# Twenty of the thirty-two rows of `wo` on each partition loaded by two GpSimd transfers of 120 partitions

## The chip, the cores and the metric

The kernel runs on one core of one Trainium2 chip. Its time is device microseconds of that core for one execution; the time before is the median of three runs. A profile is one execution of the program recorded by the hardware; its span runs from the first to the last instruction, and the execution's own time is a little longer.

The core has four engines that compute (TensorE, VectorE, ScalarE and GpSimd, in the profile PE, DVE, ACT and POOL), SyncE (SP), which here issues nearly all loads, and sixteen DMA engines that move the bytes. A transfer that SP issues is queue q1 in the profile, one that GpSimd issues is queue q0.

## The reference

One token passes an attention block over a long cache and a gated feed-forward block, side by side. All arrays are float32.

```python
x = A_x                                   # 1 x 1 x 576
xn = layernorm(x)
q = (xn @ wq).reshape(1, 1, 32, 128)      # 32 heads of 128
p = softmax(q . k_cache * 128**-0.5)      # 16384 keys a head
o = p . v_cache                           # 32 x 128
h = gelu(xn @ w_gate) * (xn @ w_up)       # 4608
out = x + o.reshape(4096) @ wo + h @ w_down
```

The two caches hold 268 MB each (32 x 16384 x 128 floats), `wo` (4096 x 576) and the three weights of the feed-forward block some 9 to 11 MB each. Every byte is used once.

## The kernel before

**Order of the work.** Lines 67 to 120 load `wq` and work out the query of all heads. Then a loop over 64 tiles of keys (two a head, 128 partitions of 64 keys) loads a tile of `k_cache` (line 178) and, three tiles later, the tile of `v_cache` that belongs to it (line 182). VectorE and ScalarE make the scores (lines 191 to 196), TensorE multiplies the probabilities with the values (line 226). The weights of the gate and of the up projection are loaded between tiles, in the first 12 of them.

**The end.** After the last tile comes the part that the change touches. Each step multiplies one column of 128 activations with 128 rows of a weight and adds into the accumulator `acc` in PSUM (`add_out`, line 297). `w_down` comes first, in three loads of 12 rows of 576 floats a partition (3456 KB each). Then the 32 x 128 attention output `oall` is transposed (line 315), copied to `orow` (line 317) and turned by a GpSimd transfer into `oT`, 128 partitions by 32 columns (line 319). Two GpSimd transfers bring `x` into `x2` (line 324). `wo` is laid out with 32 rows of 576 floats on each partition, and loaded in four pieces of 12, 12, 6 and 2 rows a partition. The piece of two rows is itself cut over the partitions into six transfers, of 8, 4, 2, 1, 112 and 1 partitions (`LAST`). Each row of a partition takes two calls of the matmul, for the two halves of 288 outputs, and each call shows as two matmuls in the profile: 48 for 12 rows, 40 for 10. Once 30 rows are in, VectorE copies half of the accumulator out (line 337) and TensorE adds it back to the other half (line 339); the last two rows follow, then `x` is added (line 342) and the result stored (line 343).

**What sets the order.** All large loads go into a ring of five buffers of 32 KB a partition, named `slot`. A load is issued when its buffer's last reader is done: the first two pieces of `wo` take the buffers of the last but one and the last tile of values, the third piece that of the first piece of `w_down`, the fourth that of the second. SP and GpSimd each issue in order; the DMA engines take what is queued, each at its own pace, and a load counts as landed when all engines that carry a share of it are done. TensorE works the pieces off in the order of the program. Where a transfer waits for nothing, the scheduler may issue it far earlier than the program has it.

Of the kernel before, what the change touches and what calls it, by code (L numbers as in the profile page):

```python
# [8 lines left out]
F32 = mybir.dt.float32  # L9
# [4 lines left out]
P = 128  # L14
H, SK, DH = 32, 16384, 128
D, DF = 576, 4608
# [12 lines left out]
HALF = D // 2  # L29
# [2 lines left out]
FQ = FS // 4  # L32
FT = FS // P
WO_T = H * DH // P
LAST = (8, 4, 2, 1, 112, 1)


@with_exitstack
def kernel(ctx: ExitStack, tc: tile.TileContext, x, k_cache, v_cache, wq, wo, wg, wu, wd, out):
    nc = tc.nc  # L40
    cpool = ctx.enter_context(tc.tile_pool(name="cpool", bufs=1))
# [9 lines left out]
    xf = x.rearrange("b s d -> (b s) d")  # L51
# [3 lines left out]
    wov = wo.rearrange("(p t) f -> p t f", t=WO_T)  # L55
    wdv = wd.rearrange("(s p t) f -> s p t f", p=P, t=FT)

    def slot():
        return slots.tile([P, R * DH], F32, tag="s", name="slot")
# [93 lines left out]
    hT = cpool.tile([P, DF // P], F32, name="hT")  # L153
# [140 lines left out]
    def add_out(j, lhs, w, last=False):  # L294
        for i in range(2):
            q = 32 * (2 * (j % 2) + i)
            nc.tensor.matmul(acc[q : q + 1, :HALF], lhs,  # L297
                             w[:, i * HALF : (i + 1) * HALF], start=q not in seen, stop=last)
            seen.add(q)

    def load_rows(src, n, cuts=(P,)):
        w = slot()[:, : n * D]
        p = 0
        for c in cuts:
            nc.sync.dma_start(w[p : p + c, :], src[p : p + c, :])
            p += c
        return w.rearrange("p (t f) -> p t f", f=D)

    for s in range(DF // FS):
        w = load_rows(wdv[s].rearrange("p t f -> p (t f)"), FT)  # L310
        for j in range(FT):
            add_out(j, hT[:, s * FT + j : s * FT + j + 1], w[:, j, :])

    po = ps_s.tile([P, 512], F32, tag="sm", name="pot")
    nc.tensor.transpose(po[:H, :P], oall, ident)
    orow = cpool.tile([H, P], F32, name="orow")
    nc.scalar.activation(orow, po[:H, :P], AF.Copy)
    oT = cpool.tile([P, WO_T], F32, name="oT")
    nc.gpsimd.dma_start(oT, orow)

    x2 = cpool.tile([P, HALF], F32, name="x2")
    nc.vector.memset(x2, 0.0)
    for i in range(2):
        nc.gpsimd.dma_start(x2[32 * i : 32 * i + 1, :], xf[:, i * HALF : (i + 1) * HALF])

    lo = 0
    for n in (12, 12, 6, 2):
        end = lo + n == WO_T
        w = load_rows(wov[:, lo : lo + n, :].rearrange("p t f -> p (t f)"), n, LAST if end else (P,))
        for j in range(n):  # L330
            add_out(0 if end else j, oT[:, lo + j : lo + j + 1], w[:, j, :],
                    last=lo + j in (WO_T - 3, WO_T - 1))
        lo += n
        if lo == WO_T - 2:
            part = cpool.tile([P, HALF], F32, name="part")
            nc.vector.memset(part, 0.0)
            nc.vector.tensor_copy(part[64:], acc[64:, :HALF])  # L337
            for i in range(2):
                nc.tensor.matmul(acc[32 * i : 32 * i + 1, :HALF], ident[:, 64 + 32 * i : 65 + 32 * i], part,
                                 start=False, stop=False)  # L340
# [31 lines left out]
```

## Time and profile before

| | |
|---|---|
| median of three runs | 1396.02 us (1395.83 to 1396.08) |
| the profiled execution | 1396.48 us |
| its span | 1394.7 us |
| bytes moved from HBM in the span | 587.60 MB |
| VectorE busy | 956.3 us |
| TensorE busy | 527.9 us |
| ScalarE busy | 536.1 us |
| GpSimd busy | 14.2 us |
| largest rate in a fortieth of the span | 438 GB/s |

The page of the profile gives first the busy time of each engine and then the span in 40 slices, with the busy share of the DMA engines in tenths and the bytes that they moved. A view by windows gives, for any stretch of the span, the busy time of an engine, the mean share of the sixteen DMA engines that was busy, and GB/s: one busy engine of sixteen is a share of 0.06. The chain of waits follows the last instruction back to what released it.

### The profile page before, as it was taken

The page shows a single profiled execution, that of the slowest core. Times are in us where ns is not written, and L with a number is a line of the kernel's source. Part 1 is how long each engine was busy: PE and PEld are TensorE (multiplying, and loading weights), DVE is VectorE, ACT ScalarE, POOL GpSimd, SP SyncE. Part 2 cuts the span into 40 slices and gives each one's busy share as a digit, 9 for nine tenths or more (in the row PEclk, how much of TensorE's full clock was granted, in tenths as well). Part 3 has the DMA queues.
Part 4 walks back from the last instruction along what each step waited for, and adds up shares of the span by engine and source line. Part 5 has one row for each costly group of instructions (what it writes and reads, how often), then busy time and mean ns, then how long its engine had stood idle before and what let it go on. Part 6 is the DMA issues. An engine that isn't in the chain of part 4 may idle for free.

```text
span 1394.7 us, 10849 instructions
## 1 busy us (share of the span) xinstructions
PE 527.9 (38%) x3071; PEld 151.4 (11%) x3071; DVE 956.3 (69%) x634; ACT 536.1 (38%) x3251; POOL 14.2 (1%) x33
## 2 busy tenths in 40 slices
PE   6634234344234323342243323332333233332575
PEld 3211001011001000000011000100011001100121
DVE  1977565739877877778777877787777777787500
ACT  0644333325443444344344434444434433443300
POOL 0000000000000000000000000000000000000000
PEclk9866667565665665656656566665666666656677
DMA  9999999999999999999999999999999999999993
GB/s 406 422 426 431 422 432 428 419 438 429 428 432 435 425 432 434 429 430 435 431 428 433 430 432 430 432 430 431 432 432 430 430 433 430 431 432 430 430 428 124
DMA packets 25618, 588.36 MB, mean 422 GB/s; under 512 B 3267, under 2 KB 3285, under 8 KB 7254
## 3 DMA queue, kind: packets, MB, share of 16 engines
q1 hardware_dynamic: 24692, 587.61, 98.4%
q8 instruction: 24, 0.39, 0.1%
q14 instruction: 36, 0.29, 0.1%
q0 software_dynamic: 864, 0.06, 0.0%
q10 hardware_dynamic: 2, 0.00, 0.0%
HBM read 587.60 MB, written 0.00 MB: 421 GB/s over the span
## 4 chain that ended last, share of the span: by engine, by line
DMA 72%; DVE 20%; PE 7%; issue 1%; POOL 0%; SPq 0%; ACT 0%; DVEq 0%
DMA slot<-in_A_k_cache_dram 34%; DMA slot<-in_A_v_cache_dram 34%; DVE slot L191 12%; DVE s L196 7%; PE po L226 5%; DMA slot<-in_A_wo_dram 3%; DMA gu<-gc 2%; PE pg L144 1%; PE acc L297 1%; POOL gu L151 0%; PE pt L206 0%; DVE pm L202 0%; PE pb L212 0%; PE pl L233 0%; SPq L63 0%
## 5 line engine op out<-in xcount | busy, mean ns | idle before, releaser
L191 DVE TENSOR_TENSOR slot<-slot,q 128x2048 f32<-128x2048 f32 x256 | 574.5, 2286 | 259.4 <-DMA slot<-in_A_k_cache_dram 259.3
L226 PE MATMUL po<-slot,pe 128*4 128x512 f32 x2048 | 372.0, 893 | 758.1 <-DMA slot<-in_A_v_cache_dram 758.1
L195 ACT ACTIVATE jk<-slot 128x128 f32<-128x128 f32 x1536 | 453.2, 296 | 521.7 <-DVE slot L191 518.5
L196 DVE TENSOR_REDUCE s<-slot 128x10 f32<-128x1280 f32 x256 | 367.7, 1478 | 0.0
L195 ACT ACTIVATION_READ_ACCUMULATOR jk<-slot 128x1 f32 x1536 | 286.8, 187 | 0.0
L226 PEld LDWEIGHTS po<-slot,pe 128*4 128x4 f32 x2048 | 60.2, 111 | 1015.7 <-DMA slot<-in_A_v_cache_dram 749.6
L245 PE MATMUL pc<-sel,o 128*128 128x1 f32 x256 | 35.3, 259 | 39.6 <-ACT o L239 39.6
L239 ACT ACTIVATE o<-po 128x512 f32<-128x512 f32 x32 | 19.0, 595 | 78.5 <-PE po L226 78.5
L214 ACT ACTIVATE nb<-pb 128x1 f32<-128x1 f32 x32 | 5.5, 171 | 95.6 <-PE pb L212 95.6
L337 DVE COPY part<-acc 64x288 f32<-64x288 f32 x1 | 0.5, 461 | 60.7 <-PE acc L297 60.7
L245 PEld LDWEIGHTS pc<-sel,o 128*128 128x128 f32 x256 | 32.6, 199 | 71.2 <-ACT o L239 71.2
L117 PE MATMUL pq<-slot,xnb 128*128 128x512 f32 x64 | 31.6, 641 | 7.9 <-DMA slot<-in_A_wq_dram 7.9
L235 DVE RECIPROCAL rl<-pl 128x1 f32<-128x1 f32 x32 | 5.4, 169 | 38.2 <-PE pl L233 38.2
L210 DVE TENSOR_REDUCE nm<-pt 1x1 f32<-1x128 f32 x32 | 8.9, 278 | 30.3 <-PE pt L206 30.3
L249 ACT ACTIVATE oall<-pc,rl 128x1 f32<-128x1 f32 x32 | 8.4, 261 | 38.2 <-PE pc L245 38.2
L144 PE MATMUL pg<-slot,xnb 128*32 128x384 f32 x192 | 21.0, 588 | 0.9 <-DMA slot<-in_B_w_up_dram 0.6
L120 ACT ACTIVATE q<-pq 128x512 f32<-128x512 f32 x8 | 4.8, 597 | 38.9 <-PE pq L118 38.9
L212 PE MATMUL pb<-nm,ones 1*128 1x1 f32 x64 | 12.0, 255 | 14.6 <-DVE nm L210 14.6
L297 PE MATMUL acc<-slot,oT 128*1 128x288 f32 x128 | 12.9, 559 | 9.8 <-DMA slot<-in_A_wo_dram 9.8
L206 PE MATMUL pt<-ident,pm 128*1 128x128 f32 x32 | 8.9, 280 | 20.0 <-DVE pm L202 19.8
L117 PEld LDWEIGHTS pq<-slot,xnb 128*128 128x128 f32 x64 | 13.2, 208 | 24.5 <-issue 24.5
L297 PE MATMUL acc<-slot,hT 128*1 128x288 f32 x144 | 12.5, 510 | 6.4 <-DMA slot<-in_B_w_down_dram 6.4
(60 smaller groups left out, 131.3 us busy)
## 6 DMA issues: line engine op xcount, KB each, us to landing
slot<-in_A_k_cache_dram SPq DMA_DIRECT2D x64, 4096.0 KB, 43.0
slot<-in_A_v_cache_dram SPq DMA_DIRECT2D x64, 4096.0 KB, 34.6
slot<-in_B_w_down_dram SPq DMA_DIRECT2D x3, 3456.0 KB, 38.0
slot<-in_B_w_gate_dram SPq DMA_DIRECT2D x3, 3072.0 KB, 43.9
slot<-in_B_w_up_dram SPq DMA_DIRECT2D x3, 3072.0 KB
slot<-in_A_wq_dram SPq DMA_DIRECT2D x2, 4096.0 KB, 14.4
slot<-in_A_wo_dram SPq DMA_DIRECT2D x2, 3456.0 KB
slot<-in_A_wo_dram SPq DMA_DIRECT2D x1, 1728.0 KB, 33.4
```

What stands on the lines that cost most here:

```text
L117: nc.tensor.matmul(pq, xnb[:, j, :], wv[:, j, g * 512 : (g + 1) * 512], start=j == 0, stop=False)
L144: nc.tensor.matmul(pg[32 * q : 32 * q + 32, :FQ], lhs, rhs, start=j == 0, stop=j == DJ)
L191: nc.vector.tensor_mul(blk, blk, Q[h].to_broadcast([P, SUB, DH]))
L195: nc.scalar.activation(jk, blk[:, n, :], AF.Copy, accum_out=S[h][:, o + n : o + n + 1])
L196: nc.vector.tensor_reduce(S[h][:, o : o + nv], blk[:, :nv, :], axis=AX.X, op=ALU.add)
L206: nc.tensor.transpose(PT[h][:1, :P], PM.pop(h), ident)
L210: nc.vector.tensor_reduce(nm, PT.pop(h)[:1, :P], axis=AX.X, op=ALU.max, negate=True)
L212: nc.tensor.matmul(pb[:, :1], ones[:1, :], nm, start=True, stop=True)
L226: nc.tensor.matmul(OP[h][q : q + 4, :], PE_[h][:, k : k + 4], vt[:, n * DH : (n + 4) * DH], start=k < 16, stop=k >= C * R - 16)
L239: nc.scalar.activation(OS[h], OP.pop(h), AF.Copy)
L245: nc.tensor.matmul(PC[h][:, :1], o4[:, j * DH : (j + 1) * DH], sel[:, j : j + 1], start=j == 0, stop=j == 3)
L297: nc.tensor.matmul(acc[q : q + 1, :HALF], lhs, w[:, i * HALF : (i + 1) * HALF], start=q not in seen, stop=last)
```

## The change

The first 20 of the 32 rows of each partition come in two loads of ten rows. Of each, GpSimd loads partitions 0 to 119 and SP the remaining eight. A row of ten is taken as two halves of five rows (11,520 bytes), kept apart in the buffer by a gap of 32 floats. Ahead of the first, between the two and behind the second stands a tiny GpSimd transfer (`turn`), which reads 2, 17 and 15 pieces of `x` into a scratch tile `pad`. The other 12 rows come by SP in loads of ten and two, now of all 128 partitions each. `pool_dma` ties each GpSimd transfer behind the GpSimd instruction that stands before it in the program; the transfers of `oT` and of `x2` are now issued through it as well.

```diff
-LAST = (8, 4, 2, 1, 112, 1)
+PART = 120
+GAP = 32
...
-    def load_rows(src, n, cuts=(P,)):
+    def load_rows(src, n):
         w = slot()[:, : n * D]
-        p = 0
-        for c in cuts:
-            nc.sync.dma_start(w[p : p + c, :], src[p : p + c, :])
-            p += c
-        return w.rearrange("p (t f) -> p t f", f=D)
+        nc.sync.dma_start(w, src)
+        w = w.rearrange("p (t f) -> p t f", f=D)
+        return [w[:, j, :] for j in range(n)]
+
+    pad = cpool.tile([P, 48], F32, name="pad")
+
+    def pool_dma(dst, src):
+        tc.keep_in_program_order(nc.gpsimd.dma_start(dst, src))
+
+    def turn(k):
+        pool_dma(pad[:k].rearrange("p (a f) -> p a f", f=16)[:, 0:3:2, :],
+                 xf[:, : k * 32].rearrange("o (k a f) -> (o k) a f", a=2, f=16))
+
+    def load_part(src, n):
+        half = n // 2 * D
+        w = slot()[:, : 2 * (half + GAP)].rearrange("p (a f) -> p a f", a=2)[:, :, :half]
+        src = src.rearrange("p (a f) -> p a f", a=2)
+        pool_dma(w[:PART], src[:PART])
+        nc.sync.dma_start(w[PART:], src[PART:])
+        return [w[:, j // (n // 2), j % (n // 2) * D : (j % (n // 2) + 1) * D] for j in range(n)]
...
-    nc.gpsimd.dma_start(oT, orow)
+    pool_dma(oT, orow)
...
-        nc.gpsimd.dma_start(x2[32 * i : 32 * i + 1, :], xf[:, i * HALF : (i + 1) * HALF])
+        pool_dma(x2[32 * i : 32 * i + 1, :], xf[:, i * HALF : (i + 1) * HALF])

     lo = 0
-    for n in (12, 12, 6, 2):
+    for n in (10, 10, 10, 2):
         end = lo + n == WO_T
-        w = load_rows(wov[:, lo : lo + n, :].rearrange("p t f -> p (t f)"), n, LAST if end else (P,))
+        src = wov[:, lo : lo + n, :].rearrange("p t f -> p (t f)")
+        if lo < 20:
+            turn(17 if lo else 2)
+            w = load_part(src, n)
+        else:
+            w = load_rows(src, n)
...
         lo += n
+        if lo == 20:
+            turn(15)
```

More of the change, by code (lines that the diff above doesn't have):

```diff
@@ L311 @@
         for j in range(FT):
-            add_out(j, hT[:, s * FT + j : s * FT + j + 1], w[:, j, :])
+            add_out(j, hT[:, s * FT + j : s * FT + j + 1], w[j])
     po = ps_s.tile([P, 512], F32, tag="sm", name="pot")
@@ L323 @@
     for i in range(2):
-        nc.gpsimd.dma_start(x2[32 * i : 32 * i + 1, :], xf[:, i * HALF : (i + 1) * HALF])
+        pool_dma(x2[32 * i : 32 * i + 1, :], xf[:, i * HALF : (i + 1) * HALF])
     lo = 0
-    for n in (12, 12, 6, 2):
+    for n in (10, 10, 10, 2):
         end = lo + n == WO_T
-        w = load_rows(wov[:, lo : lo + n, :].rearrange("p t f -> p (t f)"), n, LAST if end else (P,))
+        src = wov[:, lo : lo + n, :].rearrange("p t f -> p (t f)")
[4 more added lines that the diff above has]
+            w = load_rows(src, n)
         for j in range(n):
-            add_out(0 if end else j, oT[:, lo + j : lo + j + 1], w[:, j, :],
+            add_out(0 if end else j, oT[:, lo + j : lo + j + 1], w[j],
                     last=lo + j in (WO_T - 3, WO_T - 1))
         lo += n
+        if lo == 20:
+            turn(15)
         if lo == WO_T - 2:
```

## The prediction

> **What bounds the kernel now.** I read the slices of the page first, then the chain, then windows over the end.
>
> ```profile
> span 1394.7 us, 10849 instructions
> DMA  9999999999999999999999999999999999999993
> q8 instruction: 24, 0.39, 0.1%
> ```
>
> The DMA engines are busy in every slice but the last: transfers bound the kernel, and what this change can move lies in the last 35 us. The q8 row is instruction fetch.
>
> ```profile
> 1346.43 36.53 DMA slot<-in_A_wo_dram
> 1382.96 0.04 issue
> 1383.00 6.28 PE acc L297 x72
> 1389.28 0.02 issue
> ```
>
> The chain ends so: the second piece of `wo` lands at 1382.96, TensorE works off the 72 matmuls of the second and third piece, and from 1389.28 to 1394.7, 5.42 us, comes the fixed close (copy, add back, last two rows, add, store).
>
> ```profile
> core 0: us, PE busy (x), PEclk, DMA share, GB/s
> 1350.00:1360.00 10.00, 7.20 (x73) 0.70 1.02 433
> 1365.00:1369.00 4.00, 2.64 (x44) 1.00 0.85 252
> 1369.00:1372.00 3.00, 0.00 (x0) 0.61 0.58 220
> 1372.00:1375.00 3.00, 0.14 (x4) 0.50 0.14 48
> 1375.30:1382.40 7.10, 5.12 (x48) 0.67 0.06 24
> ```
>
> The last two columns matter: the share of sixteen DMA engines that is busy, and GB/s. Until 1360 all sixteen run, at 433 / (16 x 1.02) = 26.5 GB/s each. From 1375 the share is 0.06: one engine.
>
> ```profile
> DMA packets 33, 0.34 MB, mean 26 GB/s; under 512 B 7, under 2 KB 7, under 8 KB 18
> q1 hardware_dynamic: 32, 0.33, 5.9%
> ```
>
> This is the DMA view of 1375.3 to 1388.4: 0.33 MB through 5.9% of sixteen engines, 0.94 of one, at 26 GB/s. One engine is behind the others by 13 to 19 us (they stop between 1369 and 1375, with equal shares of each 128-row load), and TensorE waits for it. The fetched instructions are 0.39 MB, 14.7 us at 26.5 GB/s, so one engine fetching them all would fit the delay. The sum needs only that one engine is late.
>
> **The change part by part.** It aims at this engine: of twenty rows' load, 120 partitions go by GpSimd in fifteen shares of eight partitions (120 = 15 x 8), and if the engine without a share is the late one, it is relieved of two loads of ten rows.
>
> *Late engine.*
>
> ```profile
> 1364.55 3.09 PE L297 MATMUL acc<-slot,hT 128*1 128x288 f32 x48 [3.61 <-DMA slot<-in_B_w_down_dram]
> ```
>
> It delivers the last `w_down` piece at 1364.5. After that come, at worst, its share of the eight leftover partitions (2 x 23.0 KB, 1.74 us), a ten-row load (8 partitions x 23.0 KB = 184 KB, 6.95 us) and the two-row load (36.9 KB, 1.39 us): done at 1374.6, where it now needs until 1388.4. The six-way cut of the last piece goes too; on this engine that is worth two packets of 4.6 KB at most, 0.35 us.
>
> *Start of the parts.*
>
> ```profile
> 1336.45 38.51 SPq L305 DMA_DIRECT2D slot<-in_A_wo_dram  x9
> 1349.43 0.56 POOL L319 DMA_DIRECT2D oT<-orow  x1 [1055.02 <-ACT orow L317]
> 3.34 1.12 POOL L324 DMA_DIRECT2D x<-in_A_x_dram  x2 [2.03 <-DVE x L322]
> L151 POOL DMA_DIRECT2D gu<-gc x24 | 11.8, 497 | 278.2 <-ACT gc L149 278.2
> 1348.76 4.78 PE L297 MATMUL acc<-slot,hT 128*1 128x288 f32 x48
> ```
>
> Now SP issues the first piece of `wo` at 1336.45. GpSimd issues in order, and its parts stand behind `oT`, which waits for `orow` until 1349.43; the two loads of `x2`, now at 3.34, move behind it as well. So: 1349.43 + 0.56 (`oT`) + 1.12 (`x2`) + 0.50 (first turn, as a `gu` transfer) = 1351.6 for the first part. `x2` itself is wanted only in the close.
>
> ```profile
> x<-in_A_x_dram POOLq DMA_DIRECT2D x2, 1.1 KB, 5.4
> oT<-orow POOLq DMA_DIRECT2D x1, 16.0 KB, 6.4
> gu<-gc POOLq DMA_DIRECT2D x24, 1.5 KB, 9.1
> ```
>
> Small GpSimd transfers land 5.4 to 9.1 us after issue. `oT` finds each engine at packets of 27.6 KB (1.04 us at 26.5 GB/s); with one ahead of its data and one ahead of its completion, 4.3 us remain. I take first data at 1355, between 1353.5 and 1358. The other engines finish `w_down` 13 to 19 us before the late one, at 1345 to 1351, so they stand idle for 4 to 10 us, but for the leftover partitions, which cost nothing there. SP's ten-row load follows when TensorE frees a buffer at 1348.76 + 4.78 = 1353.54: also ready by about 1355.
>
> *Second part.* The 17-row turn rewrites what the first turn wrote, so it waits for that landing, and the second part and the last turn are queued behind it on GpSimd. The first turn is issued at 1351.1 and lands at 1360.2 by the 9.1 us row; the second part's data begin some 4 us after its issue, at 1365. Until then the fifteen engines have the first part and the ten-row load, 13.9 us from 1355. So the wait is covered to 1369; without that cover it would cost its full excess.
>
> *Pace, no collisions.* Each of the fifteen engines carries 3 x 6.95 + 1.39 = 22.2 us, and the second part lands at 1377.2.
>
> *Pace with collisions.* No row shows a transfer of 120 partitions, so I bound it by the nearest ones. A full 128-partition load is the kind end: the 433 GB/s above. The other end is the cut piece, in flight in the windows 1365 to 1372:
>
> ```profile
> slot<-in_A_wo_dram SPq DMA_DIRECT2D x1, 504.0 KB, 24.2
> slot<-in_A_wo_dram SPq DMA_DIRECT2D x1, 36.0 KB
> ```
>
> There the engines are busy but slow: 16 x (0.85 x 4 + 0.58 x 3) = 82 engine-us for 252 x 4 + 220 x 3 = 1668 KB, which at 26.5 GB/s are 63. The 19 lost ones fall on about 0.54 MB (112 + 8 + 4 + 2 + 1 partitions of 4.6 KB, less the late engine's share), themselves 20 engine-us: each byte of a transfer dealt otherwise than over 128 partitions costs itself again, 0.95 times. I take doubling for the two parts, because the 112-partition piece is the nearest row and eight partitions a share are likewise not the deal of a full load: 5.53 MB over 15 x 26.5 GB/s are 13.9 us more. The second part then lands at 1391.1. Both ends, 0 and 13.9 us, stay for the range.
>
> The Trainium skill, "SBUF — State Buffer", section "Door 1: The DMA port swizzle", gives a reason: four neighbouring partitions, and those 32 further on, share one of sixteen DMA ports, each about as fast as one engine. By that rule engines with the first and the fifth run of eight partitions write through the same port at once; the sum would be the doubled one. The 252 GB/s at 0.85 agree.
>
> *TensorE behind it.*
>
> ```profile
> 1374.86 5.57 PE L297 MATMUL acc<-slot,oT 128*1 128x288 f32 x48 [7.21 <-DMA slot<-in_A_wo_dram]
> ```
>
> After the second part come 80 matmuls (two ten-row pieces). At the chain's pace, 6.28 / 72, they take 6.98 us; at that of the row above (clock about half) 9.3, at that of the `w_down` row (3.09 for 48) 5.2. I take 6.98. The close stays 5.42.
>
> *Sum.* 1391.1 + 0.04 + 6.98 + 5.42 = 1403.5 us of span against 1394.7: 8.8 more. The profiled execution took 1396.48, 1.78 more than its span, and 0.46 more than the median of 1396.02. Forecast: 1396.02 + 8.8 = **1404.8 us**.
>
> **The rivals.**
>
> *No collisions.* The parts run as full loads do. For it: fifteen engines at 26.5 GB/s could do it, and the late engine is relieved as intended. Against it: the stretch above. 1377.2 + 12.44 = 1389.6 of span, 5.1 less: 1390.9 us. This is the other side. Its price is the collision alone: the sides change where collisions cost 5.1 us, that is 0.37 of the parts' own 13.9 us.
>
> *Half collisions.* Engines that share rows drift apart, so that one is at its own rows while the other is at the common ones: 6.5 us more instead of 13.9 gives 1397.4. For it: two engines half a share apart don't meet. Against it: all start together, from idle, at 1355.
>
> *The wrong engine is left out.* Then the change doesn't do what it says. The late engine goes on from 1364.5 with 3 x 6.95 + 1.39, and perhaps 1.74: done at 1386.7 to 1388.5, a span of 1399.1 to 1400.9, so 1400.4 to 1402.2; if its last part collides too, up to 1416. No view numbers the engines, and nothing in the trace shows a GpSimd transfer on fewer than sixteen. The Trainium skill, "DMA: Bandwidth & Descriptors", section "Why a DMA increments its semaphore by 16 and not by 1", says that such a transfer takes as many consecutive engines as divide its row counts, from a cursor that moves on; 2, 15, 1 (for 17), 15 and 15 make 48, three rounds, and both parts would leave out the second engine. By its exception for some plain copies the parts would sit on engines 0 to 14, the second one included: this rival's time. No run here shows either.
>
> **How the numbers follow.** Collisions in full 0.55, around 1404.8, from 1400 (0.6 of them) to 1411 (half as much again). Half collisions 0.13, of which 0.10 within the band of no change. No collisions 0.22, 1389.5 to 1393. Wrong engine 0.10. The range 1390.0 to 1412.0 takes all but the edges: some 0.05 of the rival without collisions, 0.04 of the wrong engine, 0.07 of full collisions. The likeliest case alone spans 1400 to 1411. A measurement of this kernel tells about 0.2%, 2.8 us, from no change. Faster than that: 0.22. Within: 0.10. Slower: 0.68.
>
> **What would show it.** GB/s fall well under 433 between 1345 and 1355, while GpSimd issues its first part at about 1351.6: the late start. Between 1356 and 1390 the DMA share is near 0.9 and GB/s between 200 and 300: collisions; near 400 means none, and the forecast is wrong by the 13.9 us. After 1375 no stretch with a share of 0.06 at 26 GB/s: the late engine is relieved; if one stays, to 1388 or longer, another was left out. TensorE's last wait ends with a `slot<-in_A_wo_dram` from GpSimd near 1391, with 80 matmuls behind it. If that landing comes near 1391 and the end does not come 12.4 us later, the TensorE term is wrong. If GpSimd's second part is issued after 1366, its wait was not covered.

## The result and the profile after

The changed kernel takes 1413.66 us (median of four runs, 1412.51 to 1414.82) against 1396.05 us (1395.83 to 1396.32) for the kernel before on the same chip: 1.0126 times as long, interval 1.0109 to 1.0144. The profiled execution took 1414.82 us, its span 1413.0 us. The direction was forecast, the size was not: 17.6 us were lost where the forecast had 8.8, and the time lies 1.7 us above the range.

First the page of the profile after: the span, and the slices of DMA share and of GB/s.

```profile
span 1413.0 us, 10858 instructions
...
DMA  9999999999999999999999999999999999999995
GB/s 401 427 425 427 430 426 426 426 431 430 430 430 431 430 431 430 429 431 433 433 430 430 431 430 432 431 430 430 432 429 431 431 430 431 431 430 429 431 234 114
```

The last of these rows was, before:

```profile
GB/s 406 422 426 431 422 432 428 419 438 429 428 432 435 425 432 434 429 430 435 431 428 433 430 432 430 432 430 431 432 432 430 430 433 430 431 432 430 430 428 124
```

In the first 38 slices the two rows agree within 8 GB/s. In the last two the engines stay busy (9, then 5) while GB/s fall to 234 and 114. The loss is in the end of the kernel and in its transfers. The windows over that end give the stages; columns are the length, TensorE's busy time with its instructions, its granted clock, the busy share of the DMA engines, and GB/s.

```profile
core 0: us, PE busy (x), PEclk, DMA share, GB/s
1348.00:1352.00 4.00, 3.65 (x36) 0.73 0.55 176
1352.00:1356.00 4.00, 2.26 (x28) 0.84 0.66 146
1356.00:1366.00 10.00, 4.74 (x40) 0.53 1.04 235
1366.00:1376.00 10.00, 1.13 (x12) 0.67 0.98 226
1376.00:1386.00 10.00, 5.19 (x48) 0.67 1.00 220
1386.00:1396.00 10.00, 4.31 (x40) 0.67 1.04 209
1396.00:1400.00 4.00, 0.00 (x0) 0.50 0.19 36
```

Read the two last columns together. From 1348 to 1356 the share is 0.55, then 0.66, and the rate low: engines have nothing to do, the late start that was forecast. From 1356 to 1396 the share is 1.0 and the rate 209 to 235 GB/s, where before a share of 1.02 went with 433: the engines are all busy and move about half as much. The DMA view of 1356 to 1396 parts this by queue (packets, MB, and the time that the packets took as a share of sixteen engines).

```profile
q0 software_dynamic: 518, 5.06, 58.7%
q1 hardware_dynamic: 301, 3.82, 42.6%
```

At 26.5 GB/s an engine (the prediction's figure), GpSimd's 5.06 MB need 191 us of engine time. They took 0.587 x 16 x 40 = 376: 185 more, 0.97 of their own. SP's 3.82 MB need 144 and took 273: 129 more, 0.90 of their own. Those 129 us are the ones the forecast did not have.

The chain of waits after ends so:

```profile
1352.75 0.77 POOL slot L311
1353.52 13.31 issue
...
1367.81 32.30 DMA slot<-in_A_wo_dram
...
1400.15 7.20 PE acc L298 x80
```

GpSimd issues the first part at 1352.75, waits 13.3 us for the first turn's landing, and issues the second at 1367.81. It lands at 1400.11, and 80 matmuls and the close follow. TensorE's own rows show what became of the late engine:

```profile
1376.29 5.19 PE L298 MATMUL acc<-slot,hT 128*1 128x288 f32 x48 [9.15 <-DMA slot<-in_B_w_down_dram]
```

The last piece of `w_down`, worked off from 1364.55 before, is in only at 1376.29. The list of packets in the trace shows whose delay this is. The last ten packets of `w_down`, of 27.6 KB each, follow one another without a gap from 1355.9 to 1375.5, so they are taken as one engine's; no packet of a part stands between them, and each takes 1.96 us on average where such a packet took 1.03 before. The engine that was to be relieved has no share of the parts, as intended, but has become 11.7 us later with a load that the change does not touch.

### The profile page after: what moved, and what is told of

Same layout as the page of the kernel before. It is cut to its first block, busy times and chain, and to the rows that moved or that the text cites. A ratio compares the mean times of both kernels' runs of the same rounds, so it can differ in the third digit from the quotient of the medians.

```text
span 1413.0 us, 10858 instructions
## 1 busy us (share of the span) xinstructions
PE 521.3 (37%) x3071; PEld 149.9 (11%) x3071; DVE 956.2 (68%) x634; ACT 536.0 (38%) x3251; POOL 17.8 (1%) x38
## 4 chain that ended last, share of the span: by engine, by line
DMA 73%; DVE 18%; PE 6%; issue 2%; POOL 0%; SPq 0%; ACT 0%; DVEq 0%; POOLq 0%
DMA slot<-in_A_k_cache_dram 36%; DMA slot<-in_A_v_cache_dram 23%; DVE slot L192 11%; DVE s L197 7%; DMA slot<-in_B_w_gate_dram 6%; PE po L227 3%; DMA slot<-in_B_w_up_dram 3%; DMA slot<-in_A_wo_dram 2%; DMA slot<-in_B_w_down_dram 2%; DMA gu<-gc 2%; PE pg L145 1%; PE acc L298 1%; POOL gu L152 0%; DVE pm L203 0%; PE pt L207 0%
## 5 line engine op out<-in xcount | busy, mean ns | idle before, releaser
L227 PE MATMUL po<-slot,pe 128*4 128x512 f32 x2048 | 364.8, 877 | 765.6 <-DMA slot<-in_A_v_cache_dram 765.6
L298 PE MATMUL acc<-slot,hT 128*1 128x288 f32 x144 | 15.8, 619 | 16.2 <-DMA slot<-in_B_w_down_dram 16.2
L152 POOL DMA_DIRECT2D gu<-gc x24 | 12.0, 505 | 279.8 <-ACT gc L150 279.8
```

What stands on the lines that cost most here:

```text
L152: nc.gpsimd.dma_start(gu[32 * q : 32 * q + 32, which, s * FT : (s + 1) * FT], gc[32 * q : 32 * q + 1, :])
L227: nc.tensor.matmul(OP[h][q : q + 4, :], PE_[h][:, k : k + 4], vt[:, n * DH : (n + 4) * DH], start=k < 16, stop=k >= C * R - 16)
L298: nc.tensor.matmul(acc[q : q + 1, :HALF], lhs, w[:, i * HALF : (i + 1) * HALF], start=q not in seen, stop=last)
```

## The experiments

Three theories were set against each other. A: the writes collide; by the rule quoted in the prediction the partitions have a few ways in, four neighbours and the four that stand 32 further on share one, and engines that use the same one at once get half the pace each. B: GpSimd's queue is slow with pieces of this size. C: the late start and the waits between the turns leave engines idle. All ratios below are against the kernel before on the same chip, with their intervals.

### The parts through SP, and over all partitions

`sp120` takes the parts of 120 partitions through SP and leaves the turns out.

```diff
-        pool_dma(w[:PART], src[:PART])
+        nc.sync.dma_start(w[:PART], src[:PART])
...
-            turn(17 if lo else 2)
...
-        if lo == 20:
-            turn(15)
```

> The changed kernel with the two parts of 120 partitions issued by SP in place of GpSimd, and without the tiny transfers. Theory A: the deal over 120 partitions stays, so the stretch after 1345 us runs at 200 to 260 GB/s with the engines busy, and the time is 1405 to 1420 us. Theory B: with GpSimd gone the stretch runs near 400 GB/s and the time is 1391 to 1398. Theory C: SP issues both parts by 1347 us, so 1391 to 1398 as well.

Measured: 1427.67 us, 1.0226 (1.0209 to 1.0243): on the side of theory A, but 7.7 us above the stretch given for it.

`gp128` keeps GpSimd and the turns, but loads all 128 partitions in each part.

```diff
-        pool_dma(w[:PART], src[:PART])
-        nc.sync.dma_start(w[PART:], src[PART:])
+        pool_dma(w, src)
```

> The changed kernel with each ten-row part over all 128 partitions by GpSimd, nothing left over for SP; the tiny transfers and their waits stay. Theory A: if GpSimd deals 128 partitions as SP does, the stretch runs near 400 GB/s, the late engine is not relieved, and the time is 1396 to 1401 us, about that of the kernel before. Theory B: the parts still crawl, 1408 us or more. Theory C: start and waits are unchanged, so 1408 or more as well.

Measured: 1402.79 us, 1.0045 (1.003 to 1.006): 1.8 us above the stretch given for A, and 5 below what B and C asked for. A window of `sp120`, then those of `gp128` and its DMA view of 1356 to 1376:

```profile
1356.00:1366.00 10.00, 0.02 (x4) 0.61 1.00 200
```

```profile
1356.00:1366.00 10.00, 5.19 (x48) 0.67 1.00 426
1366.00:1376.00 10.00, 5.18 (x48) 0.67 1.00 409
1376.00:1386.00 10.00, 4.98 (x40) 0.50 0.08 30
```

```profile
q0 software_dynamic: 517, 5.33, 63.3%
q1 hardware_dynamic: 257, 3.01, 36.4%
```

The slow pace goes with the 120 partitions, not with GpSimd: SP at 120 has 200 GB/s, GpSimd at 128 has 409 to 426 with the same two-half form and the same turns. In `gp128` GpSimd's 5.33 MB took 0.633 x 16 x 20 = 203 us of engine time for 201, SP's 3.01 MB 116 for 114: no loss on either. Theory B falls. Against `gp128` the changed kernel loses 1413.66 - 1402.79 = 10.9 of the 17.6 us. That is what the collisions cost less what the relief gains, since loads of 128 partitions relieve no one: the last window of `gp128` has one engine left at 30 GB/s. Without collisions `gp128` is still 6.5 us slower than before, and that lies in the order of the work: its second part lands at 1387.53 instead of 1382.96, with 80 matmuls (7.39 us) behind it instead of 72 (6.28).

`gp128` also shows whose fault the late `w_down` was:

```profile
1367.51 5.18 PE L298 MATMUL acc<-slot,hT 128*1 128x288 f32 x48 [5.06 <-DMA slot<-in_B_w_down_dram]
```

Without collisions the last `w_down` piece is in at 1367.5, with them at 1376.3. In `gp128` the late engine carries a share of the first part besides, so at least these 8.8 us of its delay are collisions on the ways in that it uses too.

### The parts ahead of `oT`

`early_parts` issues the turns and parts before the transpose, each turn with a scratch tile of its own, so that nothing waits.

```diff
-    pad = cpool.tile([P, 48], F32, name="pad")
+        pad = cpool.tile([P, 48], F32, name=f"pad{k}")
...
+    parts = []
+    for k in (2, 17):
+        turn(k)
+        a = 10 * len(parts)
+        parts.append(load_part(wov[:, a : a + 10, :].rearrange("p t f -> p (t f)"), 10))
+    turn(15)
...
-            turn(17 if lo else 2)
-            w = load_part(src, n)
+            w = parts[lo // 10]
...
-        if lo == 20:
-            turn(15)
```

> The changed kernel with both parts and the tiny transfers put ahead of the transfer of oT on GpSimd, and the tiny ones writing to separate tiles, so that nothing waits for orow or for a tiny transfer. Theory A: parts start at 1337 and 1347 us, the idle stretch before 1355 goes, but the collisions stay: 1400 to 1409 us. Theory C: all that was lost was the start: 1393 us or less. Theory B: as theory A.

Measured: 1416.77 us, 1.0142 (1.0127 to 1.0157), 7.8 us above the stretch given for A. GpSimd's timeline and one window:

```profile
1337.24 0.77 POOL L310 DMA_DIRECT2D slot<-in_A_wo_dram  x1 [1043.96 <-DMA slot<-in_A_wo_dram]
...
1345.19 0.74 POOL L310 DMA_DIRECT2D slot<-in_A_wo_dram  x1 [6.22 <-PE po L227]
```

```profile
1348.00:1356.00 8.00, 3.15 (x28) 0.59 0.99 213
```

The parts start 15 and 22 us earlier and the idle windows are gone (a share of 0.99 from 1348 to 1356 instead of 0.55 to 0.66), yet the kernel is no faster, where C asked for 1393 us or less: theory C falls as the cause of the loss. A colliding load that starts earlier only slowed earlier what ran beside it: TensorE gets the last piece of `w_down` at 1382.36 instead of 1376.29.

### Another engine left out

`other_engine` changes only the sizes of the turns, 5, 17 and 12 instead of 2, 17 and 15.

```diff
-            turn(17 if lo else 2)
+            turn(17 if lo else 5)
-            turn(15)
+            turn(12)
```

> The changed kernel with turns of 5, 17 and 12 pieces in place of 2, 17 and 15, so that, if a turn of k pieces moves the first engine of the next part by k (by 1 for 17), both parts leave out the fifth engine and the late one gets a share of each. Theory A (rows collide) with turns that work: the late engine carries two more shares of 184 KB, 13.6 us at its own pace and about twice that while others write to the same rows, so 1425 to 1442 us. If the turns don't choose the engines: no difference from the changed kernel, 1411 to 1416.

Measured: 1423.26 us, 1.0196 (1.0179 to 1.0213), 9.6 us above the changed kernel and 1.7 us below the expected stretch. One of its windows:

```profile
1396.00:1406.00 10.00, 4.98 (x40) 0.50 0.07 27
```

One engine is left alone for some ten us, and the second part lands at 1408.57; in the changed kernel no such stretch remains (0.19 from 1396 to 1400, and the landing at 1400.11). So the turns do steer which engine stays without a share, and, with the packets of `w_down` above, the change leaves out the one that it means to. The rival of the wrong engine falls. This agrees with the cursor that the Trainium skill describes ("DMA: Bandwidth & Descriptors", "Why a DMA increments its semaphore by 16 and not by 1"): a turn of five instead of two moves the parts' first engine on by three.

### Loads one at a time, by partition range

`probe_ranges` leaves out all computation: sixteen loads of ten rows of `wo` a partition, each alone on the engines.

> This kernel leaves all of the computation out: it only loads ten rows of wo a partition (23,040 bytes) sixteen times, each after the one before has landed and been read, over different partitions and from SP or GpSimd; its output is not the block's. Theory A (rows collide: four neighbouring partitions and those 32 further on take data at about one engine's pace, whoever sends it): SP over partitions 0 to 127 lands 7 us plus 2 to 3 us of latency after its issue; 0 to 63 and 64 to 127 take as long with half the bytes, about 9 us, while 32 to 95, as many bytes, takes 6; 0 to 119 takes 14 to 17; 40 to 95 takes 6. GpSimd the same, with 40 to 95 and 32 to 91 at 6 to 7 us and 0 to 59 at 9 to 10. Theory B (GpSimd's queue moves large pieces slowly): all SP transfers go by bytes, 0 to 63 as fast as 32 to 95, 0 to 119 under 10 us, and all GpSimd ones take twice as long as SP's. Theory C (late start and waits) says nothing here: no transfer differs but by bytes.

One window inside the transfer of each load, columns as above (no engine computes): SP with partitions 0 to 127, 0 to 63, 32 to 95, 64 to 127 and 0 to 119, then GpSimd with 0 to 127 and with 0 to 119 in two halves.

```profile
12.50:19.00 6.50, 1.00 0.91 383
22.70:30.00 7.30, 1.00 0.94 202
33.00:37.20 4.20, 1.00 0.86 329
39.50:46.50 7.00, 1.00 0.96 204
50.00:64.00 14.00, 1.00 0.81 173
85.00:92.50 7.50, 1.00 0.98 387
107.50:121.00 13.50, 1.00 0.90 195
```

The first four rows settle it. 64 partitions from 0 or from 64 run at 202 to 204 GB/s, 64 partitions from 32 at 329, with the engines about as busy (shares of 0.94, 0.96 and 0.86). What counts is not how many partitions but which lie together: 0 to 31 with 32 to 63 get in one another's way, 32 to 63 with 64 to 95 don't. SP and GpSimd agree at 128 (383, 387) and are both slow at 120 (173, 195). GpSimd's loads of 60 partitions, later in the same run, agree: VectorE waits 10.1 us for partitions 0 to 59 and 6.5 us for 32 to 91. The rule of the Trainium skill quoted in the prediction ("SBUF — State Buffer", "Door 1: The DMA port swizzle") says just this: four partitions and the four that stand 32 further on share one of sixteen ports. By it 0 to 63 reach eight ports, and eight times an engine's 26.5 GB/s are 212; the trace has 202. The 120 partitions from 0 to 119 lie on all sixteen by the same rule. For their slow pace this probe shows no reason; that shares of eight partitions which stand four apart meet is the prediction's argument, on which `aligned56` below bears.

### Loads two and three at a time

`probe_pairs` sets parts and full loads beside each other, again without the computation, and times `oT` with and without loads beside it.

> All computation of the reference is left out; the kernel only loads ten rows of `wo` a partition, now two loads at a time, and copies the 16 KB of `orow` into `oT`, with and without two full loads beside. It asks why the collisions cost half as much again as the parts' own time, and 13.9 us were forecast for once. Alone, a full load of 2.88 MB took 8.2 us and a part of 120 partitions 14.3 us. Theory A (rows that share one way in, each at about one engine's pace) has two forms. A1: only the part's bytes cost double, and the full load beside it runs at its own pace; then a part of 120 partitions beside a full load takes about 14.3 + 8.2 = 22.5 us or less, and two parts of 120 together 28.6 us. A2: the full load beside it is slowed as well, since its rows are written by the part's engines too; then part and full load together take 25 us or more. For reference two full loads together should take 16.3 us, at 360 GB/s or more. Theory on the turn: a part of 56 partitions (40 to 95, 1.26 MB) on the fourteen engines that also write these rows for the full load beside it ends with it after some 12 us; without the turn ahead of it, on engines two further, 14 to 18 us. `oT` through ScalarE's queue: theory that its small packets wait one by one behind the large ones gives some 3 us alone and 15 us or more beside two full loads, through GpSimd 4 us alone and 6 to 9 us beside them; the rival, that ScalarE's queue is slow by itself, gives 15 us or more alone too.

VectorE touches each load once it has landed. Its timeline for a full load and a part of 120 partitions (released at 47.7), then for two parts (released at 72.2):

```profile
47.46 0.23 DVE L73 TENSOR_TENSOR slot<-mark 128x1 f32<-128x1 f32 x2
62.92 0.15 DVE L81 COPY mark<-slot 128x1 f32<-128x1 f32 x1 [15.23 <-DMA slot<-in_A_wo_dram]
71.79 0.15 DVE L81 COPY mark<-slot 128x1 f32<-128x1 f32 x1 [8.71 <-DMA slot<-in_A_wo_dram]
71.98 0.23 DVE L73 TENSOR_TENSOR slot<-mark 128x1 f32<-128x1 f32 x2
...
103.15 0.15 DVE L81 COPY mark<-slot 128x1 f32<-128x1 f32 x1 [13.62 <-DMA slot<-in_A_wo_dram]
```

Two parts take 30.9 us. The pair takes 24.1 us, between form A1 (22.5, only the part costs double) and A2 (25 or more). The queues in the windows 5 to 19 (two full loads) and 49.5 to 62.7 (the pair, while both run):

```profile
q1 hardware_dynamic: 271, 5.55, 92.7%
```

```profile
q1 hardware_dynamic: 128, 2.58, 60.2%
q0 software_dynamic: 128, 1.23, 34.3%
```

A full load beside another full load takes 0.927 x 16 x 14 = 208 us of engine time for 5.55 MB, which need 209. Beside a part it takes 127 for 2.58 MB, which need 97: 0.31 more. So a colliding transfer does slow a full load that uses the same ways in.

The part of 56 partitions (40 to 95) beside a full load ended after 12.8 us with the turn ahead of it and after 14.1 without: the expected order, though both numbers lie close together. The queue of SP took 99 us of engine time for 99 with the turn (21.5 to 32.5) and 117 for 102 without (34.5 to 46.5): which engine writes which partitions counts, but for little in this pair.

`probe_triples` asks for the size with more in flight.

> All computation of the reference is left out; three loads of ten rows of `wo` a partition at a time, five sets: three full loads; two parts of 120 partitions and a full load; one part and two full loads; two parts alone; two GpSimd loads of all 128 partitions and a full load. It asks for the size of the slowdown that the full load beside the parts takes. By rows: a part's packets are busy for 209 us of engine time alone, 105 more than its bytes need at 26.5 GB/s, and a full load needs 111. If only the part's bytes cost double (A1), two parts and a full load are 2 x 209 + 111 = 529 us of engine time, 34 us on fifteen and a half engines. If the full load is slowed as in the pair measured before (150 for 111), 568, or 36.6 us. If it is slowed as in the changed kernel (272 for 144, 0.9 of its own), 2 x 209 + 210 = 628, or 40.5 us. One part and two full loads: 431, 510 or 629 us, that is 27.8, 33 or 40.6 us. Two parts alone: 30.9 us as before. The loads of 128 partitions, by both queues: 333, or 21 to 24.5 us.

Two parts and a full load ended 38.3 us after their release, one part and two full loads 32.7, two parts alone 31.1, three loads of 128 partitions 23.2. The queues in one part with two full loads (68 to 81), then two parts alone (102 to 129):

```profile
q1 hardware_dynamic: 147, 3.02, 73.3%
q0 software_dynamic: 99, 1.04, 26.4%
```

```profile
q0 software_dynamic: 535, 5.34, 94.0%
```

The full loads took 152 us of engine time for 114, again a third more. The one full load beside two parts took 115 for 89 (30 to 64), 0.29 more. Parts alone took 406 for 202: their own once more, 1.01 times. The triple with two parts is above A1 (34), nearer to the size measured in the pair (36.6) than to that of the changed kernel (40.5); the triple with one part meets the pair's (33, where A1 has 27.8 and the changed kernel's size 40.6). In the kernel SP's loads lost 0.9 of their own, in these probes 0.29 to 0.34.

### The same relief without collisions

If theory A holds, the late engine can be relieved by a transfer whose engines are each meant to keep to a way in of their own. `aligned56` lays `wo` out anew: 2048 rows over 128 partitions by SP (12 and 4 rows), 1792 rows over partitions 40 to 95 by GpSimd (parts of 14, 14 and 4 rows, `turn(2)` ahead of each, meant to leave the part to the fourteen engines that also fill these rows in a full load), 256 rows over 128 partitions. `oT` goes through ScalarE's queue.

```diff
+    T1, T2, LO, HI = 16, 32, 40, 96
+    wo1 = wo[: P * T1].rearrange("(p t) f -> p t f", t=T1)
+    wo2 = wo[P * T1 : P * T1 + (HI - LO) * T2].rearrange("(p t) f -> p t f", t=T2)
+    wo3 = wo[P * T1 + (HI - LO) * T2 :].rearrange("(t p) f -> p t f", p=P)
...
+        turn(2, lo)
...
+        pool_dma(w[LO:HI, :, :half], src)
...
-    pool_dma(oT, orow)
+    nc.scalar.dma_start(oT1, orow[:T1])
+    nc.scalar.dma_start(oT2[LO:HI], orow[T1:30])
```

> A kernel laid out anew after theory A. wo is cut into 2048 rows over 128 partitions by SP (16 a partition), 1792 rows over partitions 40 to 95 by GpSimd (32 a partition, in parts of 14, 14 and 4) and 256 rows over 128 partitions by SP. Over 56 partitions a share is four neighbouring partitions, no two shares have common rows, and with a turn of 2 ahead of each part fourteen engines without the late one carry them, each into the rows that it also fills in a full load; the rows of the late engine get nothing from a part. Theory A: after w_down at 1364.5 us the late engine has 18 rows a partition left, 12.3 us, and ends at 1377; with 16 matmuls and the close the time is 1383 to 1389 us. If relieving the late engine is worth nothing, or if GpSimd's queue is what costs: 1394 or more.

Measured: 1398.48 us, 1.0012 (1.0003 to 1.0021), 9.5 us above its expected stretch. The chain names the cause:

```profile
1351.19 18.75 DMA oT<-orow
...
1370.08 19.69 PE acc L298 x287
```

`oT` lands 18.75 us after its issue, and TensorE then has 287 matmuls in a row to do. `aligned56_no_turn` drops the turns:

```diff
-        turn(2, lo)
```

> The kernel over 56 partitions without the turns: the same rows, but, if the turns choose the engines, parts on the first fourteen engines, the late one among them. Theory A with turns that work: the late engine carries 32 rows of four partitions more, 10.9 us, so 1391 to 1399 us. If turns don't matter: as with them.

Measured: 1408.01 us, 1.0083 (1.0066 to 1.0099), 9.5 us more than with them and 9 above the expected stretch. One window with the turns, then without:

```profile
1348.00:1352.00 4.00, 3.19 (x29) 0.78 1.03 433
1348.00:1352.00 4.00, 0.00 (x0) 0.65 0.96 251
```

The loads and their partitions are the same in both kernels; only the engines that carry the parts differ. With the turns SP's queue took 209 us of engine time for 210 between 1344 and 1364, and GpSimd's 97 for 96: no loss. Without them SP's took 224 for 152, 0.47 more, and GpSimd's 91 for 55, 0.67 more. So what collides is not a range of partitions by itself but the way the engines are set to it. The 9.5 us were expected from the late engine's load alone; but `oT`, too, lands 29.65 us after its issue instead of 18.75, and TensorE waits for it.

`aligned56_v2` keeps the turns, gives `oT` back to GpSimd, and lets TensorE do the second piece of `w_down` ahead of the first part.

```diff
-    nc.scalar.dma_start(oT1, orow[:T1])
-    nc.scalar.dma_start(oT2[LO:HI], orow[T1:30])
+    pool_dma(oT2[32:HI], orow[14:30])
+    pool_dma(oT1, orow[:T1])
...
-    add_rows(r1, oT2[:HI], 0)
     add_rows(wds[1], hT, FT)
...
+    add_rows(r1, oT2[:HI], 0)
     add_rows(wds[2], hT, 2 * FT)
```

> The kernel over 56 partitions, with oT now turned by GpSimd (as in the kernel before, where that landed in 6.4 us) in place of ScalarE's queue, where it took 19 us and held TensorE until 1370 us, and with the second w_down piece ahead of the first part on TensorE. In the run before the parts themselves kept the engines at 390 to 430 GB/s and the late engine's last 128-row piece landed at 1374.5. Theory A: with that wait gone the late engine ends near 1377 and the time is 1383 to 1390 us, below both kernels. If the relief is not real: 1394 or more.

Measured: 1387.78 us (1387.31 to 1391.1), 0.9943 (0.9929 to 0.9956): within its expected stretch, 8.7 us faster than the kernel before on the same chip, 26 faster than the change. Windows, and one piece of the chain:

```profile
1356.00:1366.00 10.00, 8.18 (x93) 0.66 0.91 369
1366.00:1372.00 6.00, 4.22 (x72) 1.00 0.92 373
1372.00:1376.00 4.00, 4.00 (x75) 1.00 0.40 154
1376.00:1380.00 4.00, 4.00 (x68) 1.00 0.03 12
```

```profile
1371.59 8.47 PE acc L298 x136
```

A share of 0.91 goes with 369 GB/s, 25 GB/s an engine, and the engines are busy until 1372 and nearly all done by 1376: no stretch of 13 us with one engine is left. From 1371.59 on TensorE bounds, with 136 matmuls without a gap. How much of the 8.7 us is the relief and how much the new order of the work was not separated.

## Why the prediction was wrong in size

*Late engine.* Forecast done at 1374.6 with everything. It had not even finished `w_down` then (1376.3), though it carries no share of the parts, as forecast. The step counted its bytes at 26.5 GB/s and did not see that other engines write through its way in: its packets took 1.96 us instead of 1.03, and `gp128` puts at least 8.8 us on that.

*Start of the parts.* Forecast issue at 1351.6, measured 1352.75; right. The engines' idle time is there in the windows, but shorter than the 4 to 10 us forecast: shares of 0.55 and 0.66 over 4 us each leave 3.2 us of all sixteen.

*Second part.* Forecast issue at about 1361, measured 1367.81. The first turn came in late among the slow packets (it landed 14.8 us after issue instead of the 9.1 taken from the `gu` row; in `gp128` 9.6). The wait left no engines idle: the share is 1.04 from 1356 to 1366. The test set for this, an issue after 1366, was the wrong one, since collisions stretch the cover together with the wait.

*Pace with collisions: the step that failed.* It priced the parts' bytes at twice their own time, 13.9 us. For the parts this was right: 0.97 of their own measured in the kernel, 1.01 in the probe with two parts. But it let SP's loads beside them run at full pace. They took 129 us of engine time more, 129 / 16 = 8.1 us, and the landing came 1400.11 - 1391.1 = 9.0 us late. The row was there: between 1365 and 1372, beside the cut piece of before, the step found 19 us of engine time lost and charged all of it to the cut piece's bytes. The list of packets in that trace says otherwise. The cut piece's 101 packets (4.6 KB) took 0.24 us each instead of 0.17, 7 us in all; the other 12 fell on full loads beside it, 71 packets of 13.8 KB at 0.66 instead of 0.52 and 8 of 27.6 KB at 1.28 instead of 1.04. So the term that the step put at nothing stood in its own row. And the doubling of the parts, right as it came out, did not follow from that row, where the cut piece lost 0.4 of its own: there the step was lucky.

That full loads are slowed by a colliding one is shown by the pair, the triples and `aligned56_no_turn`. How much is not settled: 0.29 to 0.34 of their own in the probes, 0.47 in `aligned56_no_turn`, 0.9 in the kernel. Two parts in flight do not make the difference (0.29 in the triple), nor do the late engine's `w_down` or the load of two rows: from 1366 to 1376 SP's queue moved nearly only packets of its ten-row load (67 packets, 1.53 MB), the same load as in the probes, and took 107 us of engine time for 58, 0.85 more. In `other_engine`, with the same transfers by other engines, SP's queue lost 0.63 (232 us for 142, from 1356 to 1396). So the size differs with the engines that meet; what sets it was not tried and stays open.

*TensorE and the close.* 7.20 us for 80 matmuls against 6.98, and 5.65 us for the close against 5.42. Right within 0.5 us.

*The rivals.* No collisions: false, and where there are none (`gp128`) the kernel is still 6.5 us slower than before, with all sixteen engines carrying the parts. Half collisions: false; the engines do not drift into a phase that spares them: two parts alone lose 1.01 of their own over 27 us. The wrong engine: false by `other_engine`.

## What to carry to other kernels

Read the DMA share and GB/s of a stretch together: busy engines at half the rate meant here that transfers met on the same ways into the partitions, and neither an earlier issue nor another queue mended it; another range of partitions, with the engines that fit it, did. Before cutting a load over partitions, ask which engine writes where and who else writes there at that time, and charge the loss to both. Relieving a late engine of its share of one transfer is not enough if others then write where its remaining loads go.

## What the runs showed of the hardware that was not expected

`oT` is 16 KB in small pieces. Through ScalarE's queue it took 18.75 us in `aligned56`, there cut in two transfers; through GpSimd's queue it landed 6.4 us after issue before. `probe_pairs` repeats it beside two full loads, ScalarE's first and GpSimd's second:

```profile
179.42 0.15 DVE L81 COPY mark<-oT 128x1 f32<-128x1 f32 x1 [11.69 <-DMA oT<-orow]
195.58 0.15 DVE L81 COPY mark<-oT 128x1 f32<-128x1 f32 x1 [6.63 <-DMA oT<-orow]
```

VectorE waited 11.7 and 6.6 us. Alone the two waits were 1.96 and 2.05 us: in this probe ScalarE's queue was not slow by itself, only with large loads under way. Each case ran once, and why GpSimd's queue is hit less was not tried.
